# Softmax steps given out one at a time, and four values visits joined to the next scores, in a two-layer attention kernel

## The chip, the cores and the metric

The kernel runs on one core of a Trainium2 chip. The metric is device microseconds of one execution. The kernel before takes 1779.6 us, the median of three runs (1779.0 to 1781.2).

## The reference

Two attention layers of the same size (S = 2048 positions, D = 1024, 32 heads of 32) are computed from separate inputs, and their outputs are put side by side.

```python
# layer A: each position sees 8 positions back, every second one
qkv = (x @ wqkv).reshape(B, S, 3, H, Dh); q, k, v = ...      # H = 32, Dh = 32
off = jnp.arange(8) * 2
idx = pos[:, None] - off[None, :]
logits = einsum("bhsd,bhswd->bhsw", q, k[idx]) * Dh**-0.5     # masked where idx < 0
o = einsum("bhsw,bhswd->bhsd", softmax(logits), v[idx])
a = o.reshape(B, S, D) @ wo
# layer B: each position sees the 256 positions up to itself
scores = einsum("bhqd,bhkd->bhqk", q, k) * Dh**-0.5           # masked to 0 <= q - k < 256
b = einsum("bhqk,bhkd->bhqd", softmax(scores), v).reshape(B, S, D) @ wo
return concatenate([a, b], axis=-1)
```

## The kernel before

The work is cut into eight units of 512 positions: u0 to u3 are layer B, u4 to u7 layer A. For layer A the even and the odd positions are laid out as separate rows, so that "every second position" becomes a plain window of neighbours. A unit has eight groups (s0 to s7) of four heads. In the names below, u5s0 is the first group of unit 5.

Most of TensorE's time goes into three GEMMs: queries and keys (`qk_items`, matmuls at L616), values (`v_items`, L685) and the output projection (`o_items`, L749). Each number is kept as a high and a low part, and each product takes three matmuls, so matmuls come in multiples of three. A weight tile `raw` is loaded by a DMA that POOL issues (L182). Its high half is a cast, on ScalarE (L233) or on VectorE (L236), and its low half is a subtract on VectorE, two instructions of 128x512 (L239). GEMM outputs go to PSUM banks g (two of them) and x (one), and are read out from there before the bank is used again.

In layer A a group is handled by `window(u, s)`. SyncE gathers its queries and keys with eight DMAs into `pbuf` (L536). A *scores visit* of TensorE is 32 pairs of small matmuls into the four banks s (L822, 64 rows of the profile). Then comes the softmax, on a tile `band`, of which there are two, used in turn:

- VectorE adds the mask, four instructions, one for each bank (L830);
- VectorE takes the maximum (L840) and subtracts it (L842), ScalarE takes the exponential (L846);
- VectorE sums (L854), takes the reciprocal (L856), multiplies (L858), and transposes two halves (L861) into a tile `wide`;
- ScalarE copies each half into strips, four pairs of copies each (L870, L873).

A *values visit* (L896) multiplies the strips with the values of `vbuf`, one half of the rows into the bank o and the other half into a bank s. Where the table `PAIRS` names two groups, their two values visits follow each other without a break. In `overlap`, ScalarE and VectorE add what the two halves share (L994, L996), form the high and low parts (L998 to L1007), and give the banks back. A wide round of the values GEMM, 48 matmuls for two banks at a time, stands at a unit's first group.

No engine's order is found while the kernel runs: each engine executes its instructions in the order in which the program was written. A planner writes it. It keeps a model of every engine's time (`Clock`, named `ck`): `ck.use(engine, duration, ready)` books an instruction and returns its end, and `ck.defer(t, f)` has `f` called, and its instructions written, when the model's TensorE reaches time `t`. TensorE's work is a set of four queues of items; the planner takes the item that can start first by its `ready()`. Weight splits are written as the GEMM items ask for them. A function that writes several instructions at once therefore puts them next to each other on their engine, and whatever is written later stands behind them all:

```python
nc.vector.reciprocal(sm, sm)
ck.use("dve", 0.285, ck.now)
nc.vector.tensor_tensor(p16(), p16(), sm[...], op=ALU.mult)
ck.use("dve", 1.39, ck.now, port=True)
for i in range(2):
    nc.vector.transpose(turned[i], band[buf][:, 768 * i:768 * i + 768])
    e = ck.use("dve", 0.88, ck.now)
    ck.defer(e - 0.1, lambda i=i, e=e: spread(i, e))
```

Of the kernel before, what the change touches and what calls it, by code (L numbers as in the profile page):

```python
# [9 lines left out]
AF = mybir.ActivationFunctionType  # L10
# [4 lines left out]
P = 128  # L15
# [245 lines left out]
def kernel(ctx, tc, xs, wqk, wv, wo, outs, units):  # L261
# [531 lines left out]
    def window(u, s):  # L793
# [13 lines left out]

        h = pairs[hg % 2] = {}
# [29 lines left out]
        def top():  # L838
            nm = small.tile([P, 16], F32, tag="nm", name="nm")
            nc.vector.tensor_reduce(nm, p16(), axis=mybir.AxisListType.X, op=ALU.max)  # L840
            ck.use("dve", 1.39, ck.now)
            nc.vector.tensor_tensor(p16(), p16(), nm[:, :, None].to_broadcast([P, 16, 72]), op=ALU.subtract)  # L842
            e = ck.use("dve", 1.39, ck.now, port=True)

            def expo():
                nc.scalar.activation(p16(), p16(), AF.Exp)  # L846
                e2 = ck.use("act", 1.07, e)
                ck.defer(e2 - 0.1, lambda: total(e2))

            ck.defer(e - 0.1, expo)  # L850

        def total(e):
            sm = small.tile([P, 16], F32, tag="sm", name="sm")
            nc.vector.tensor_reduce(sm, p16(), axis=mybir.AxisListType.X, op=ALU.add)  # L854
# [3 lines left out]
            nc.vector.tensor_tensor(p16(), p16(), sm[:, :, None].to_broadcast([P, 16, 72]), op=ALU.mult)  # L858
            ck.use("dve", 1.39, ck.now, port=True)
            for i in range(2):  # L860
                nc.vector.transpose(turned[i], band[buf][:, 768 * i:768 * i + 768])  # L861
                e = ck.use("dve", 0.88, ck.now)
                ck.defer(e - 0.1, lambda i=i, e=e: spread(i, e))

        def spread(half, e):
            pieces = turned[half].rearrange("p (j b t c) -> p j b t c", j=2, b=4, t=3)
            diag = wide[buf][:, 2 * half:2 * half + 2].rearrange("p j (b c) -> p j b c", b=4)
            for i in range(4):
                r, c = 32 * i, 32 * i + 8
# [4 lines left out]
                t = ck.use("act", 0.255, e)  # L874
            if half:
                h["p"] = t + PACE[u][3] + HOLD[u][s]

        def values_ready():
            if len(seats_x.free) < len(both):
                return None  # L880
            return latest(done["v"].get((u, vp)), *[x.get("p") for x in both], ro.when(),
                          rs.when() if alone else rs.empty())

        def values():
            own = ro if alone or s % 2 else rs
            h["o"], first_bank = own.take()
            h["o2"], bank = rs.take()
            halves = [h["o"], h["o2"]]
# [11 lines left out]

            return lambda: overlap(u, s, h, bank, own, first_bank, 0 if has_halo else 1)

# [79 lines left out]

    def overlap(u, s, h, bank, own, first_bank, first):

# [363 lines left out]
```

## Time and profile before

| | |
|---|---|
| median of three runs | 1779.6 us |
| the profiled execution | 1781.06 us, its span 1779.3 us |
| TensorE matmuls (PE) | 1766.2 us busy, 99% |
| TensorE weight loads (PEld, beside PE) | 1474.0 us, 83% |
| VectorE (DVE) | 1260.9 us, 71% |
| ScalarE (ACT) | 1048.8 us, 59% |
| GpSimd (POOL) | 375.4 us, 21% |
| DMA | 257.51 MB, mean 145 GB/s |

Times in the profile are microseconds from the start of the span. A row of the timeline gives start, duration, engine, line, operation with its output and inputs, the shape, and how many instructions the row holds; in square brackets, the idle time before it and what ended that. The ends of matmuls are modelled, so a loss on TensorE is best read from the starts of matmuls, not from its busy share. The waits view lists for each engine what it waited for. PEclk is the clock that TensorE was granted, 1.00 being full speed. Line numbers are those of the kernel before; in the kernel after the same statements stand a little lower (L239 becomes L240, L616 L617, L685 L686, L749 L750, L822 L825, L861 L871, L896 L920).

### The profile page before, as it was taken

To read this page: it belongs to the slowest core of one execution; us is meant where nothing else is said; L and a number is where in the kernel's file an instruction comes from. 1 tells how busy PE (TensorE), PEld (TensorE's weight loads), DVE (VectorE), ACT (ScalarE), POOL (GpSimd) and SP (SyncE) were. 2 spreads that over 40 slices of the span, in tenths; PEclk is the share of its full clock that TensorE was granted. 3 is DMA by queue.
4 is the path that set the end of the run, shared out by engine and by line. 5 is a ranking of instruction groups with operands and counts; after the bars stand their busy time and mean duration, and the time that the engine had idled before them with its cause. 6 is when DMAs were issued, how large, how long until landed. Compare 5 with 4: busy or idle time off the path is not lost.

```text
span 1779.3 us, 39469 instructions
## 1 busy us (share of the span) xinstructions
PE 1766.2 (99%) x15210; PEld 1474.0 (83%) x15210; DVE 1260.9 (71%) x2690; ACT 1048.8 (59%) x2629; POOL 375.4 (21%) x829
## 2 busy tenths in 40 slices
PE   9999999999999999999999999999999999999999
PEld 7888888888888888888888888877888888888897
DVE  5678776677676779665766578776678676957873
ACT  5677766765776666676666455644455445534452
POOL 3322323224222212232233300110001100110000
PEclk9999999999999999999999999999999999999999
DMA  6656655647555556545554443433444443544432
GB/s 207 159 149 174 175 139 151 161 136 207 151 156 162 146 151 185 141 141 139 144 162 123 137 137 120 154 120 125 139 121 141 145 129 119 156 142 126 130 104 83
DMA packets 109723, 257.51 MB, mean 145 GB/s; under 512 B 14560, under 2 KB 29920, under 8 KB 109536
## 3 DMA queue, kind: packets, MB, share of 16 engines
q0 software_dynamic: 41760, 152.06, 28.5%
q1 hardware_dynamic: 58560, 86.15, 18.4%
q10 hardware_dynamic: 9216, 16.78, 2.5%
q8 instruction: 120, 1.97, 0.5%
q14 instruction: 67, 0.55, 0.1%
HBM read 164.63 MB, written 23.07 MB: 105 GB/s over the span
## 4 chain that ended last, share of the span: by engine, by line
PE 90%; DVE 3%; ACT 2%; DMA 2%; issue 2%; POOL 0%; SPq 0%; DVEq 0%; ACTq 0%; POOLq 0%
PE g L616 30%; PE g L749 16%; PE g L685 14%; PE x L616 6%; PE s L1121 6%; PE s L1037 5%; PE o L1186 3%; PE x L749 3%; PE x L685 2%; PE s L822 1%; PE x L1186 1%; DVE w L239 1%; PE s L896 1%; DMA raw<-wv 1%; DMA raw<-xs 1%
## 5 line engine op out<-in xcount | busy, mean ns | idle before, releaser
L616 PE MATMUL g<-x,w 128*128 128x512 f32 x2568 | 639.3, 392 | 0.6 <-ACT w L233 0.6
L616 PEld LDWEIGHTS g<-x,w 128*128 128x128 f32 x2568 | 475.4, 188 | 89.6 <-ACT w L233 1.0
L239 DVE TENSOR_TENSOR w<-raw,w 128x512 fp32r<-128x512 f32 x514 | 335.9, 695 | 42.8 <-ACT w L233 36.3
L1042 DVE CUSTOM_DVE_ANT_0 s<-s,mask_d 128x384 f32<-128x384 f32 (+2 forms) x512 | 262.7, 555 | 137.4 <-PE s L1037 136.2
L685 PE MATMUL g<-w,x 128*128 128x256 f32 (+1 forms) x1872 | 331.5, 320 | 0.7 <-DVE w L239 0.7
L1047 ACT ACTIVATE s<-s,nm 128x384 f32<-128x384 f32 (+2 forms) x512 | 274.1, 536 | 65.9 <-DVE nm L1042 64.7
L685 PEld LDWEIGHTS g<-w,x 128*128 128x128 f32 x1872 | 277.5, 191 | 24.5 <-DVE w L239 1.4
L749 PE MATMUL g<-ot,w 128*128 128x512 f32 x1200 | 294.5, 392 | 0.0
L749 PEld LDWEIGHTS g<-ot,w 128*128 128x128 f32 x1200 | 222.4, 188 | 43.4
L1106 POOL TENSOR_SCALAR_AFFINE_SELECT pbuf<-pbuf 128x128 f32<-128x128 f32 (+1 forms) x498 | 191.6, 412 | 202.5 <-ACT pbuf L1128 188.5
L1128 ACT ACTIVATE pbuf<-s 128x512 f32<-128x512 f32 (+1 forms) x368 | 188.9, 602 | 49.7 <-PE s L1121 48.1
L236 DVE CAST w<-raw 128x1024 fp32r<-128x1024 f32 x189 | 137.2, 726 | 77.9 <-PE g L616 27.3
L182 POOL DMA_DIRECT2D raw<-wqk x126 | 69.1, 549 | 505.0 <-DVE w L239 300.2
L1037 PE MATMUL s<-kst,qst 96*128 96x384 f32 (+2 forms) x512 | 141.1, 338 | 2.1 <-issue 1.0
L870 ACT COPY wide<-wide 32x256 f32<-32x256 f32 x256 | 103.4, 404 | 47.1 <-DVE wide L861 43.5
L1121 PE MATMUL s<-qst,kst 128*128 128x128 f32 (+2 forms) x704 | 126.1, 307 | 0.5 <-ACT pbuf L1128 0.3
L616 PE MATMUL x<-x,w 128*128 128x512 f32 x504 | 122.3, 393 | 0.0
L1121 PEld LDWEIGHTS s<-qst,kst 128*128 128x128 f32 x704 | 107.7, 189 | 15.8 <-ACT s L1047 1.7
L1037 PEld LDWEIGHTS s<-kst,qst 96*128 96x128 f32 x512 | 92.6, 189 | 22.6 <-ACT s L1047 3.1
L616 PEld LDWEIGHTS x<-x,w 128*128 128x128 f32 x504 | 93.3, 188 | 20.2
L1047 ACT ACTIVATION_READ_ACCUMULATOR s<-s,nm 128x1 f32 x512 | 105.9, 207 | 0.2
L182 POOL DMA_DIRECT2D raw<-wo x64 | 35.8, 559 | 322.8 <-DVE w L239 175.5
(114 smaller groups left out, 1907.5 us busy)
## 6 DMA issues: line engine op xcount, KB each, us to landing
raw<-wqk POOLq DMA_DIRECT2D x126, 512.0 KB, 4.0
raw<-wv POOLq DMA_DIRECT2D x72, 512.0 KB, 4.7
raw<-wo POOLq DMA_DIRECT2D x64, 512.0 KB, 4.1
qst<-nat SPq DMA_DIRECT2D x96, 256.0 KB, 4.1
kst<-nat SPq DMA_DIRECT2D x96, 256.0 KB, 5.2
raw<-xs POOLq DMA_DIRECT2D x28, 512.0 KB, 4.5
outs<-ost ACTq DMA_DIRECT2D x56, 256.0 KB, 2.5
kst<-halo SPq DMA_DIRECT2D x72, 128.0 KB, 2.8
```

Of the source, the lines that this page charges most:

```text
L182: self.nc.gpsimd.dma_start(raw if len(ap.shape) == 2 else raw.rearrange("p (a b) -> p a b", a=2), ap)
L236: nc.vector.tensor_copy(t[:, 0, :], raw)
L239: nc.vector.tensor_tensor(t[:, 1, c:c + 512], raw[:, c:c + 512], t[:, 0, c:c + 512].bitcast(F32), op=ALU.subtract)
L616: nc.tensor.matmul(h["ps"], h["w"][:, a, k * P:(k + 1) * P], xt[u][k][:, b, :], start=(k == 0 and i == 0), stop=(k == NK - 1 and i == 2))
L685: nc.tensor.matmul(ps, xt[u][kw * g + k][:, a, p0:p0 + P], h["w"][g][:, c, k], start=(first and t == 0 and half == 0), stop=(last and t == 2),
L749: nc.tensor.matmul(h["ps"], w[:, a, c:c + P], ot[u, k][:, b, :], start=(k == 0 and i == 0), stop=(k == NK - 1 and i == 2))
L1037: nc.tensor.matmul(ps[:, :n], q[0:96, j, b * P:(b + 1) * P], kk[0:96, j, c0:c1], start=True, stop=True)
L1042: nc.vector.tensor_tensor_reduce(ps[:, :n], ps[:, :n], mask[:, cut:full], scale=-1.0, scalar=BIG, op0=ALU.add, op1=ALU.min, accum_out=nm)
L1047: nc.scalar.activation(ps[:, :n], ps[:, :n], AF.Exp, bias=nm, scale=-1.0, accum_out=sm)
L1106: nc.gpsimd.affine_select(w, w, pattern=[[0, m], [step, n]], compare_op=ALU.is_ge, fill=0.0, base=base, channel_multiplier=chan)
L1121: nc.tensor.matmul(ps[:, x:x + w], kk[:, j, 256 + kb * P:256 + (kb + 1) * P], q[:, j, q0:q0 + w], start=True, stop=True)
L1128: nc.scalar.activation(w, ps[:, :m * n].rearrange("p (j n) -> p j n", j=m), AF.Exp)
```

## The change

Two things change, both in layer A.

*The steps.* `top` wrote maximum and subtract together; now the subtract is deferred to 0.15 us before the maximum's modelled end. `total` wrote sum, reciprocal, multiply and both transposes together; now the multiply is deferred to the end of the reciprocal, the first transpose to the end of the multiply, the second to the end of the first. `spread` wrote all eight copies of a half together; now each pair is deferred to the end of the pair before it. What the planner decides meanwhile (weight splits, read-outs of banks, another group's steps) is written between them.

*The chain.* A new table `CHAIN` names a group each in four places: s7 of u5, s2 and s7 of u6, s2 of u7. There the values visit waits until the next group's scores could start as well (all four s banks free, its queries and keys stacked), takes a bank g in place of a bank s for its second half, and the next group's scores follow at once.

No instruction is added or removed on any engine, and the orders of POOL and SyncE are the same.

```diff
+CHAIN = ((), (), (), (), (), (7,), (2, 7), (2,))
...
+        follows = s - 1 in CHAIN[u] if s else NG - 1 in CHAIN[u - 1]
+        leads = s in CHAIN[u]
+        h = pairs[hg % 2] = {"after": pairs[1 - hg % 2] or {}}
         def scores_ready():
-            return latest(rs.empty(), done["stack"].get((u, s)),
+            return latest(rs.empty(), done["stack"].get((u, s)), h["after"].get("run", 0.0 if not follows else None),
...
         def top():
             nc.vector.tensor_reduce(nm, p16(), axis=mybir.AxisListType.X, op=ALU.max)
-            ck.use("dve", 1.39, ck.now)
-            nc.vector.tensor_tensor(p16(), p16(), nm[:, :, None].to_broadcast([P, 16, 72]), op=ALU.subtract)
-            e = ck.use("dve", 1.39, ck.now, port=True)
+            e1 = ck.use("dve", 1.39, ck.now)
+            def less():
+                nc.vector.tensor_tensor(p16(), p16(), nm[:, :, None].to_broadcast([P, 16, 72]), op=ALU.subtract)
+                e = ck.use("dve", 1.39, ck.now, port=True)
...
+            ck.defer(e1 - 0.15, less)
...
             nc.vector.reciprocal(sm, sm)
-            ck.use("dve", 0.285, ck.now)
-            nc.vector.tensor_tensor(p16(), p16(), sm[:, :, None].to_broadcast([P, 16, 72]), op=ALU.mult)
-            ck.use("dve", 1.39, ck.now, port=True)
-            for i in range(2):
+            r = ck.use("dve", 0.285, ck.now)
+            def parts():
+                nc.vector.tensor_tensor(p16(), p16(), sm[:, :, None].to_broadcast([P, 16, 72]), op=ALU.mult)
+                ck.defer(ck.use("dve", 1.39, ck.now, port=True) - 0.15, lambda: turn(0))
+            def turn(i):
                 nc.vector.transpose(turned[i], band[buf][:, 768 * i:768 * i + 768])
                 e = ck.use("dve", 0.88, ck.now)
-                ck.defer(e - 0.1, lambda i=i, e=e: spread(i, e))
+                ck.defer(e - 0.1, lambda: spread(i, e))
+                if not i:
+                    ck.defer(e - 0.15, lambda: turn(1))
+            ck.defer(r - 0.15, parts)
...
+                if i < 3:
+                    ck.defer(t - 0.15, lambda: strip(i + 1))
...
         def values_ready():
             return latest(done["v"].get((u, vp)), *[x.get("p") for x in both], ro.when(),
+                          latest(rs.empty(), rg.when(), done["stack"].get(divmod(hg + 1, NG))) if leads else
                           rs.when() if alone else rs.empty())
         def values():
-            h["o2"], bank = rs.take()
+            other = rg if leads else rs
+            h["o2"], bank = other.take()
+            h["run"] = 0.0
...
-            rs.give(bank, e)
+            other.give(bank, e)
```

The rows of each engine's order show what moves. The first place is VectorE at the start of unit 6, where the wide round of the values GEMM runs while the softmax of the group before ends. `band` and `wide` belong to that softmax, `w` with its `raw` are weights of the round. Before:

```order
L854 TENSOR_REDUCE sm_15625<-band_11579 128x16
L856 RECIPROCAL sm_15625<-sm_15625 128x16
L858 TENSOR_TENSOR band_11579<-band_11579,sm_15625 128x16x72
L861 STREAM_TRANSPOSE wide_11312<-band_11579 128x768
L861 STREAM_TRANSPOSE wide_11581<-band_11579 128x768
L239 TENSOR_TENSOR w_15646<-raw_15539,w_15646 128x512 x2
L236 CAST w_15678<-raw_15590 128x1024
```

After:

```order
L861 TENSOR_REDUCE sm_15558<-band_11579 128x16
L863 RECIPROCAL sm_15558<-sm_15558 128x16
L524 MEMSET nat_15511 128x8
L867 TENSOR_TENSOR band_11579<-band_11579,sm_15558 128x16x72
L240 TENSOR_TENSOR w_15597<-raw_15522,w_15597 128x512 x2
L871 STREAM_TRANSPOSE wide_11312<-band_11579 128x768
L1020 TENSOR_TENSOR o_15613<-o_15613,band_11310 128x8x8
L237 CAST w_15661<-raw_15527 128x1024
L240 TENSOR_TENSOR w_15661<-raw_15527,w_15661 128x512 x2
```

The split of the round's weight (`w_15646` before, `w_15597` after) stood behind both transposes; now it stands ahead of them, and the next weight's cast and split follow between the two.

The second place is TensorE at the edge from unit 4 to unit 5. The rows `s<-pbuf` are scores visits, `g<-w,x` the wide round. Before, the scores of u5s0 stand inside that round:

```order
L896 MATMUL s<-wide,vbuf_124 32x64 x4
L616 MATMUL x<-x,w 128x512 x6
L685 MATMUL g<-w,x 128x512 x36
L822 MATMUL s<-pbuf 64x72 x32
L685 MATMUL g<-w,x 128x512 x12
L685 MATMUL x<-w,x 128x512 x3
```

After, the scores that come first here are those of u4s6 and u4s7:

```order
L686 MATMUL g<-w,x 128x256 x6
L825 MATMUL s<-pbuf 64x72 x32
L617 MATMUL g<-x,w 128x512 x12
L825 MATMUL s<-pbuf 64x72 x32
L617 MATMUL g<-x,w 128x512 x12
L617 MATMUL x<-x,w 128x512 x24
L686 MATMUL g<-w,x 128x512 x48
```

and the scores of u5s0 come later, in the next group's queries and keys:

```order
L686 MATMUL x<-w,x 128x512 x3
L686 MATMUL g<-w,x 128x512 x3
L617 MATMUL g<-x,w 128x512 x3
L825 MATMUL s<-pbuf 64x72 x32
L617 MATMUL g<-x,w 128x512 x6
```

The scores of u5s0 move behind the rest of the values GEMM, 63 GEMM matmuls and one values visit later relative to the start of the round, and the scores of u4s7 stand 12 matmuls behind those of u4s6.

VectorE at that second place, after, from the subtract of u4s6 on; `band_11310` is the softmax of u4s6 and `band_11579` that of u4s7:

```order
L847 TENSOR_TENSOR band_11310<-band_11310,nm_13314 128x16x72
L240 TENSOR_TENSOR w_13389<-raw_13295,w_13389 128x512 x2
L843 TENSOR_REDUCE nm_13393<-band_11579 128x16
L861 TENSOR_REDUCE sm_13405<-band_11310 128x16
L863 RECIPROCAL sm_13405<-sm_13405 128x16
L847 TENSOR_TENSOR band_11579<-band_11579,nm_13393 128x16x72
L867 TENSOR_TENSOR band_11310<-band_11310,sm_13405 128x16x72
L240 TENSOR_TENSOR w_13441<-raw_13352,w_13441 128x512 x2
L861 TENSOR_REDUCE sm_13449<-band_11579 128x16
L863 RECIPROCAL sm_13449<-sm_13449 128x16
L871 STREAM_TRANSPOSE wide_11312<-band_11310 128x768
L240 TENSOR_TENSOR w_13462<-raw_13367,w_13462 128x512 x2
```

The steps of the two groups alternate, and the weights of the round (`w_13389`, `w_13441`, `w_13462`) stand between them, where before one group's steps stood as blocks.

The third place is TensorE at u7s2, one of the four places in `CHAIN`. Before, nine GEMM matmuls stand between the values (L896) and the next scores (L822):

```order
L896 MATMUL o<-wide,vbuf_123 32x72 x4
L896 MATMUL s<-wide,vbuf_123 32x64 x4
L616 MATMUL x<-x,w 128x512 x9
L822 MATMUL s<-pbuf 64x72 x32
L616 MATMUL x<-x,w 128x512 x6
L749 MATMUL g<-ot,w 128x512 x42
```

After, the scores follow the values at once, and the values write to a bank g:

```order
L920 MATMUL g<-wide,vbuf_123 32x72 x4
L920 MATMUL o<-wide,vbuf_123 32x72 x4
L920 MATMUL g<-wide,vbuf_123 32x64 x4
L825 MATMUL s<-pbuf 64x72 x32
L750 MATMUL g<-ot,w 128x512 x24
L750 MATMUL x<-ot,w 128x512 x12
```

More of the change, by code (lines that the diff above doesn't have):

```diff
@@ L840, in top, with expo @@
             nc.vector.tensor_reduce(nm, p16(), axis=mybir.AxisListType.X, op=ALU.max)
-            ck.use("dve", 1.39, ck.now)
-            nc.vector.tensor_tensor(p16(), p16(), nm[:, :, None].to_broadcast([P, 16, 72]), op=ALU.subtract)
-            e = ck.use("dve", 1.39, ck.now, port=True)
[L845 to L850, printed above, removed]
+            e1 = ck.use("dve", 1.39, ck.now)
+            def less():
+                nc.vector.tensor_tensor(p16(), p16(), nm[:, :, None].to_broadcast([P, 16, 72]), op=ALU.subtract)
+                e = ck.use("dve", 1.39, ck.now, port=True)
+                def expo():
+                    nc.scalar.activation(p16(), p16(), AF.Exp)
+                    e2 = ck.use("act", 1.07, e)
+                    ck.defer(e2 - 0.1, lambda: total(e2))
+                ck.defer(e - 0.1, expo)
+            ck.defer(e1 - 0.15, less)
         def total(e):
@@ L867, in spread, with strip @@
             diag = wide[buf][:, 2 * half:2 * half + 2].rearrange("p j (b c) -> p j b c", b=4)
-            for i in range(4):
+            def strip(i):
                 r, c = 32 * i, 32 * i + 8
@@ L874, in spread @@
                 t = ck.use("act", 0.255, e)
-            if half:
-                h["p"] = t + PACE[u][3] + HOLD[u][s]
+                if i < 3:
+                    ck.defer(t - 0.15, lambda: strip(i + 1))
+                else:
+                    h["strips"] = h.get("strips", 0) + 1
+                    if h["strips"] == 2:
+                        h["p"] = t + PACE[u][3] + HOLD[u][s]
+            strip(0)
         def values_ready():
@@ L899, in values @@
                     seen.add((i, j))
-            return lambda: overlap(u, s, h, bank, own, first_bank, 0 if has_halo else 1)
+            return lambda: overlap(u, s, h, bank, other, own, first_bank, 0 if has_halo else 1)
         alone = s // 2 not in PAIRS[u]
@@ L980, in join, with overlap @@
         ck.defer(r, add)
-    def overlap(u, s, h, bank, own, first_bank, first):
+    def overlap(u, s, h, bank, other, own, first_bank, first):
         hg = u * NG + s
```

1 line of the change is left out of this document (removed).

## The prediction

> **What bounds the kernel now.** I read the page's head first, then the waits of TensorE, then the timeline around each wait they show. The page:
>
> ```profile
> span 1779.3 us, 39469 instructions
> PE 1766.2 (99%) x15210; PEld 1474.0 (83%) x15210; DVE 1260.9 (71%) x2690; ACT 1048.8 (59%) x2629; POOL 375.4 (21%) x829
> ```
>
> TensorE (PE) is busy for 1766.2 of 1779.3 us. No other engine is near that, and the change takes no instruction away, so it can gain only what PE loses, in one of three forms: a wait, a stretch in which its matmuls run slower than elsewhere, or the switch from one kind of matmul to another. The waits view of PE, whose columns are what it waited for, us in total, times, and the longest, holds these rows in layer A:
>
> ```profile
> PE x L685 <- DVE w L239: 1.6, 1, 1.6
> PE s L896 <- issue: 1.0, 1, 1.0
> PE g L685 <- DVE w L239: 0.7, 2, 0.4
> ```
>
> So PE waits for a weight's low half (L239, VectorE) three times and once for nothing that the profile shows. Waits alone understate the loss, so I also measure each place against the pace of undisturbed GEMM, which the timeline of PE gives (start, us, engine, line, operation, count):
>
> ```profile
> 1245.31 5.60 PE L749 MATMUL x<-ot,w 128*128 128x512 f32 x24
> 1250.75 4.24 PE L749 MATMUL g<-ot,w 128*128 128x512 f32 x18
> ```
>
> 24 matmuls take 1250.75 − 1245.31 = 5.44 us, 0.2267 each. A visit to the window attention is dearer than its matmuls' own time, since PE changes kind twice. The two visits at u7s2/s3 price it:
>
> ```profile
> 1642.79 2.20 PE L616 MATMUL x<-x,w 128*128 128x512 f32 x9
> 1645.76 2.33 PE L616 MATMUL x<-x,w 128*128 128x512 f32 x9
> 1648.02 0.94 PE L822 MATMUL s<-pbuf 32*64 32x72 f32 x64
> 1648.89 1.65 PE L616 MATMUL x<-x,w 128*128 128x512 f32 x6
> ```
>
> From 1642.79 to 1648.89 are 6.10 us with 18 GEMM matmuls (4.08) in them: 2.02 for a values visit and a scores visit, about 1.01 each.
>
> **The change part by part.** *Unit u5's first group.* PE at the edge from u4 to u5, then SyncE's queue, ScalarE and VectorE, then two rows of the table by windows (length, busy time of PE, PEld, DVE, ACT, POOL, granted clock, DMA share, GB/s):
>
> ```profile
> 1158.08 8.32 PE L685 MATMUL g<-w,x 128*128 128x512 f32 x36
> 1166.33 0.34 PE L822 MATMUL s<-pbuf 32*64 32x72 f32 x4
> 1168.62 0.50 PE L685 MATMUL g<-w,x 128*128 128x512 f32 x1
> 1169.37 4.37 PE L685 MATMUL g<-w,x 128*128 128x512 f32 x11 [0.26 <-DVE w L239]
> 1173.58 0.85 PE L685 MATMUL x<-w,x 128*128 128x512 f32 x3
> ```
>
> ```profile
> 1155.59 8.58 SPq L536 DMA_DIRECT2D pbuf<-nat  x8
> ```
>
> ```profile
> 1162.72 1.05 ACT L233 CAST w<-raw 128x1024 fp32r<-128x1024 f32 x1
> ```
>
> ```profile
> 1166.31 1.84 DVE L861 STREAM_TRANSPOSE wide<-band 128x768 f32<-128x768 f32 x2
> 1168.07 1.25 DVE L239 TENSOR_TENSOR w<-raw,w 128x512 fp32r<-128x512 f32 x2
> ```
>
> ```profile
> 1166.33:1169.90 3.57, 2.48 (x68) 1.80 (x68) 3.57 (x6) 2.50 (x8) 0.02 (x1) 1.00 0.14 37
> 1169.90:1173.30 3.40, 3.40 (x9) 2.65 (x9) 3.33 (x5) 3.22 (x10) 0.53 (x1) 0.50 0.53 154
> ```
>
> From 1158.08 to 1173.58 are 15.50 us. In them lie 48 matmuls (10.88) and one scores visit (1.07 with its share of the last, longer triplet): 3.55 are lost, in three ways. The gather that feeds these scores (L536) was still being issued until 1164.17, and PE stalls inside the visit. Then the weight whose cast ended at 1163.77 gets its low half only at 1168.07, since the softmax of the other group stands ahead of it on VectorE as one block that ends with the two transposes. Then the clock is halved for 3.40 us, which costs 1.7: it follows a stretch in which PE was busy 2.48 of 3.57 us.
>
> [...]
>
> In the new order these scores stand 63 GEMM matmuls and one visit later relative to the round of values GEMMs (L685): 63 × 0.2267 + 1.01 = 15.3 us, against a gather that was late by about 1. The first stall goes: −3.55 with what followed it. What is late next: the round itself now runs 48 matmuls without a visit, four weights of 12, while two groups' softmaxes (u4s6 and u4s7, now 12 matmuls apart) share VectorE with those weights. From the end of u4s7's scores to the last weight's low half VectorE has, in the new order, four masks (0.4 each, an estimate: a quarter of the elements of the multiply quoted for u6 below), three reduces (1.37), two subtracts and a multiply (1.39 each, with the gap to the next step), two reciprocals (0.3), one transpose (0.92) and three splits (1.3): 1.6 + 4.1 + 4.2 + 0.6 + 0.9 + 3.9 = 15.3. PE asks for that weight 72 matmuls after the scores, 16.3. A cover of 1.0, from which any wait of VectorE for the exponentials is taken; between 0 and the whole 3.55 I take +0.5.
>
> *Unit u6's first group.* The timeline of PE, ScalarE and VectorE:
>
> ```profile
> 1360.43 0.39 PE L685 MATMUL x<-w,x 128*128 128x512 f32 x1
> 1362.40 0.73 PE L685 MATMUL x<-w,x 128*128 128x512 f32 x2 [1.58 <-DVE w L239]
> ```
>
> ```profile
> 1355.73 1.06 ACT L233 CAST w<-raw 128x1024 fp32r<-128x1024 f32 x1
> ```
>
> ```profile
> 1356.28 1.34 DVE L854 TENSOR_REDUCE sm<-band 128x16 f32<-128x1152 f32 x1
> ...
> 1357.94 1.36 DVE L858 TENSOR_TENSOR band<-band,sm 128x1152 f32<-128x1152 f32 x1
> 1359.33 1.84 DVE L861 STREAM_TRANSPOSE wide<-band 128x768 f32<-128x768 f32 x2
> 1361.10 1.25 DVE L239 TENSOR_TENSOR w<-raw,w 128x512 fp32r<-128x512 f32 x2
> ```
>
> PE's next matmul starts 1362.40 − 1360.43 = 1.97 late less one pace, 1.74. The cast ended at 1356.79; the low half waited for reduce, reciprocal, multiply and both transposes, 4.8 us. In the new order the low half stands ahead of the transposes: it would run from 1359.33 to 1360.6, and PE asks at 1360.66. Gain 1.74. Behind it the next weight has a transpose (0.92), a small addition (64 elements a partition, taken as no longer than ScalarE's 0.40 for 256, quoted further below), its cast (no longer than ScalarE's 1.06) and its low half (1.25) to go, 3.6 us at most, and PE asks for it 12 matmuls (2.72) on. Ends 0 and 0.9, taken +0.4.
>
> *Unit u7's first group*, the same pattern, smaller:
>
> ```profile
> 1554.33 0.39 PE L685 MATMUL g<-w,x 128*128 128x512 f32 x1
> 1555.14 0.73 PE L685 MATMUL g<-w,x 128*128 128x512 f32 x2 [0.43 <-DVE w L239]
> ```
>
> 1555.14 − 1554.33 − 0.23 = 0.58, and it goes: −0.58.
>
> *The wait without a releaser*, in a visit for two groups' values in u5:
>
> ```profile
> 1222.04 0.92 PE L896 MATMUL s<-wide,vbuf 64*32 64x8 f32 x76
> 1224.77 0.30 PE L896 MATMUL s<-wide,vbuf 64*32 64x64 f32 x4 [1.04 <-issue]
> 1225.01 3.06 PE L749 MATMUL g<-ot,w 128*128 128x512 f32 x12
> 1268.15 6.28 PE L749 MATMUL g<-ot,w 128*128 128x512 f32 x27
> 1274.37 0.92 PE L896 MATMUL s<-wide,vbuf 64*32 64x8 f32 x76
> 1275.94 5.05 PE L749 MATMUL g<-ot,w 128*128 128x512 f32 x21
> ```
>
> The visit took 1225.01 − 1222.04 = 2.97 and its twin 1275.94 − 1274.37 = 1.57: 1.40 lost. Nothing released it, so I read it as PE's own instructions not being there, which the page's queue 8 carries:
>
> ```profile
> q8 instruction: 120, 1.97, 0.5%
> ```
>
> 1.97 MB in 120 packets is 16 KB a packet. Such a stall would hang on where the long visit falls in the stream, and in the new order this visit starts 12 instructions further on. Of the long visits of this kernel this one alone shows it, so I book −1.40; its other end is 0.
>
> [...]
>
> *The four joined visits.* The two groups' values in one run cost, from 1268.15 to 1275.94, 7.79 less 27 matmuls (6.12): 1.67, where two visits apart cost 2.02. Joining is worth 0.35 by that row, but in the new pairs the second half is scores, which read other operands; between 0 and 0.45 I take 0.3: −1.2 for four.
>
> *What the joining asks for.* The values' second half now takes a GEMM bank (g) at these places and gives it back when VectorE has formed the low half (L1004). At u5s7 and u6s7 it is taken within rounds whose tiles change bank every three matmuls (0.68), so the next g tile is due in 1.36 us. No row of before shows this; it is bounded by 0 and by the longest wait for an eviction-like step on PE, the 1.6 above. Nearer to 0, since two tiles' time covers it: +0.2 each at two places, +0.4. Behind a waiting PE all is queued. The joined values also wait for the four score banks and the next group's stack, and the scores wait for the values' turn; those scores move at most a few us and the order of SyncE's and POOL's queues is unchanged.
>
> *Steps given out singly, elsewhere.* A weight or an eviction slipped between steps makes that group's values later. The waits view shows no PE wait on the strip copies in before, so this is new cost:
>
> ```profile
> L870 ACT COPY wide<-wide 32x256 f32<-32x256 f32 x256 | 103.4, 404 | 47.1 <-DVE wide L861 43.5
> ```
>
> Between 0 and one copy of 0.40 at each of some six tightest of 25 visits (2.4), I take +0.6. The other way, a weight that comes sooner, gains nothing where PE does not wait.
>
> *Sum*, against the profiled execution's own 1781.06 (span 1779.3 and 1.76 around it): removed 3.55 + 1.74 + 0.58 + 1.40 = 7.27, joined 1.2; added 0.5 + 0.4 + 0.4 + 0.6 = 1.9. 1781.06 − 7.27 − 1.2 + 1.9 = 1774.5. That execution is 1.5 above the median of 1779.6, so a median may come out nearer 1773; I take 1774.0.
>
> **The rivals.** (1) *The edges stay late.* The round's weights are as late as before because the steps that let them through bring the second softmax in: only the joins and the 1.40 are gained, 1781.06 − 2.6 = 1778.5, within 0.2%. For it speaks the 1.0 us of cover at u5; against it u6, where the order plainly moves the split ahead. Chance 0.16.
>
> (2) *The joined visits outrun the instructions.* A joined run is nearly as long as the visit that stalled; if each of the four loses 1.4, 5.6 come back: 1774.5 + 5.6 = 1780.1, within 0.2%. Against it: the twin visit of the same length ran free. [...] Chance 0.07.
>
> (3) *Slower: half clock at all three edges.* If the two interleaved softmaxes hold a weight back by 2.5 us at each of u5, u6 and u7, and each such gap brings 1.7 of half clock as it did at 1169.90, the edges cost 3 × 4.2 = 12.6 against the 3.55 + 1.74 + 0.58 = 5.87 lost there now. With the joins and the 1.40 kept that is 1781.06 − 2.6 − 5.87 + 12.6 = 1785.2. It decides from 10.6 us at the edges (1783.2). For it: the first edge did just this. Against: the steps now let a split in between each. Chance 0.17.
>
> That the change does nothing is excluded: the order on PE has four pairs of visits adjacent that were apart.
>
> **How the numbers follow.** Forecast 0.60, rivals 0.16, 0.07 and 0.17. 0.2% of 1779.6 is 3.6 us, about what a measurement of this kernel can tell: faster means under 1776.0, slower over 1783.2. Of the forecast I leave 0.02 in the middle. Faster 0.58, same 0.25, slower 0.17. The range: downward no added cost and joins at 0.45, 1781.06 − 7.27 − 1.8 = 1772.0, and the run spread below the profiled execution (1781.06 to 1779.0) puts it at 1770.0; upward it takes in rivals 1 and 2 and the upper ends of the unknown costs, to 1781.0.
>
> **What would show it.** Right: in the profile after, no wait for L240 (the old L239) at the starts of u5, u6, u7, no half clock after the first microseconds, no gap without a releaser in a values visit, and joined visits at about 1.7 to 1.8 us. Wrong: PE waiting for a g bank behind VectorE's release at u5s7 or u6s7, PE waiting for strip copies, a granted clock under 1.00 at an edge, or a new gap in a joined visit.

## The result and the profile after

The kernel after takes 1777.73 us (median of 14 runs, 1775.36 to 1781.61), the kernel before 1780.35 (14 runs, 1778.79 to 1781.42). The medians differ by 2.6 us; the ratio is 0.9984, 95% interval 0.9977 to 0.9991. That is inside the range that was given and on the side that was forecast, but 3.7 us above the forecast of 1774.0 and inside the 0.2% called "same".

The page of the profile after, and rows of the waits of TensorE:

```profile
span 1776.3 us, 39487 instructions
PE 1764.9 (99%) x15210; PEld 1473.9 (83%) x15210; DVE 1239.7 (70%) x2662; ACT 1068.8 (60%) x2657; POOL 372.9 (21%) x829
```

```profile
PE s L920 <- ACT wide L888: 1.4, 1, 1.4
...
PE s L686 <- DVE w L240: 0.8, 1, 0.8
PE x L750 <- DVE ot L1031: 0.4, 1, 0.4
```

VectorE has 28 instructions fewer than before and ScalarE 28 more. The planner also chooses which of the two engines does a weight's cast or reads out a bank, and in the new order it gave ScalarE 18 casts and 10 read-outs more. So it isn't true, as was said ahead of the prediction, that no instruction is added or removed on any engine: VectorE is busy for 21.2 us less and ScalarE for 20.0 us more. No run holds that choice fixed, so its share in what follows is not shown.

The three waits for a weight's low half in layer A are gone (the one for L240 that is left lies at 26 us, in layer B). Two waits are new: a values visit waits for strips, and the output projection for `ot`. The timeline of TensorE shows the starts of u5, then the visit for two groups in u5, then the joined visit at the start of u6:

```profile
1160.06 11.04 PE L686 MATMUL g<-w,x 128*128 128x512 f32 x48
1170.94 0.84 PE L686 MATMUL x<-w,x 128*128 128x512 f32 x3
...
1223.03 0.92 PE L920 MATMUL s<-wide,vbuf 64*32 64x8 f32 x76
...
1224.61 1.66 PE L750 MATMUL g<-ot,w 128*128 128x512 f32 x6
```

```profile
1366.11 0.84 PE L686 MATMUL x<-w,x 128*128 128x512 f32 x3
1366.88 0.21 PE L920 MATMUL g<-wide,vbuf 64*32 64x8 f32 x4
...
1367.73 1.12 PE L825 MATMUL s<-pbuf 32*64 32x72 f32 x64
1368.78 0.96 PE L686 MATMUL g<-w,x 128*128 128x512 f32 x3
```

The 48 matmuls of u5's round start at 1160.06 and the next at 1170.94: 10.88 us, the plain pace, where the same work with one visit lost 3.55 before. The visit at 1223.03 takes 1.58 (it took 2.97). The joined visit takes from 1366.88 to 1368.78, 1.90 us; apart, values and scores take 0.84 and 0.87, 1.71. Counted from the due end of the last GEMM matmul ahead of it and with the triplet behind it, which is 0.11 longer, the joined visit costs 2.10, and two apart 2.11: no gain.

One fault of the kernel after has to be known before its time is read: in three groups of u4 some strips are copied from the next group's softmax, which the kernel before never does. The experiment "The transposes in turn" shows where, and what the time is without it.

A measure that recurs below is *layer A*: the time from the start of the first scores visit to the start of the last matmul. In the profile before it is 753.85 us, in the profile after 749.43.

### The profile page after: what moved, and what is told of

Its sections match the earlier page's. It is cut to its first block, busy times and chain, and to the rows that moved or that the text cites. A ratio compares the mean times of both kernels' runs of the same rounds, so it can differ in the third digit from the quotient of the medians.

```text
span 1776.3 us, 39487 instructions
## 1 busy us (share of the span) xinstructions
PE 1764.9 (99%) x15210; PEld 1473.9 (83%) x15210; DVE 1239.7 (70%) x2662; ACT 1068.8 (60%) x2657; POOL 372.9 (21%) x829
## 3 DMA queue, kind: packets, MB, share of 16 engines
q8 instruction: 120, 1.97, 0.5%
## 4 chain that ended last, share of the span: by engine, by line
PE 95%; ACT 2%; DVE 1%; DMA 1%; issue 0%; POOL 0%; SPq 0%; POOLq 0%; ACTq 0%; DVEq 0%
PE g L617 32%; PE g L686 16%; PE g L750 15%; PE s L1145 6%; PE x L617 6%; PE s L1061 5%; PE x L750 4%; PE o L1210 3%; PE x L686 3%; PE s L825 2%; PE x L1210 1%; PE s L920 1%; PE o L920 1%; ACT s L1071 0%; ACT qst L1106 0%
## 5 line engine op out<-in xcount | busy, mean ns | idle before, releaser
L617 PE MATMUL g<-x,w 128*128 128x512 f32 x2640 | 656.8, 392 | 1.0 <-ACT w L234 1.0
L617 PEld LDWEIGHTS g<-x,w 128*128 128x128 f32 x2640 | 488.8, 188 | 92.8 <-ACT w L234 1.5
L240 DVE TENSOR_TENSOR w<-raw,w 128x512 fp32r<-128x512 f32 x514 | 335.7, 695 | 52.7 <-ACT w L234 46.5
L750 PE MATMUL g<-ot,w 128*128 128x512 f32 x1128 | 276.6, 392 | 0.0
L750 PEld LDWEIGHTS g<-ot,w 128*128 128x128 f32 x1128 | 209.2, 188 | 40.6
L237 DVE CAST w<-raw 128x1024 fp32r<-128x1024 f32 x176 | 128.1, 728 | 68.4 <-PE g L617 24.9
L617 PE MATMUL x<-x,w 128*128 128x512 f32 x432 | 103.6, 392 | 0.0
L183 POOL DMA_DIRECT2D raw<-wv x72 | 46.3, 643 | 255.3 <-DVE w L240 123.3
```

Of the source, the lines that this page charges most:

```text
L183: self.nc.gpsimd.dma_start(raw if len(ap.shape) == 2 else raw.rearrange("p (a b) -> p a b", a=2), ap)
L237: nc.vector.tensor_copy(t[:, 0, :], raw)
L240: nc.vector.tensor_tensor(t[:, 1, c:c + 512], raw[:, c:c + 512], t[:, 0, c:c + 512].bitcast(F32), op=ALU.subtract)
L617: nc.tensor.matmul(h["ps"], h["w"][:, a, k * P:(k + 1) * P], xt[u][k][:, b, :], start=(k == 0 and i == 0), stop=(k == NK - 1 and i == 2))
L750: nc.tensor.matmul(h["ps"], w[:, a, c:c + P], ot[u, k][:, b, :], start=(k == 0 and i == 0), stop=(k == NK - 1 and i == 2))
```

## The experiments

Each kernel was timed beside runs of the kernel before; times below are medians, and layer A is from the one profiled execution.

| kernel | time, us | ratio to before, 95% | layer A, us |
|---|---|---|---|
| before; again | 1780.35; 1780.1 (one run) | | 753.85; 751.49 |
| after; again | 1777.73; 1778.10 | 0.9984 (0.9977 to 0.9991); 0.9983 (0.9974 to 0.9991) | 749.43; 749.11 |
| steps only | 1778.04 | 0.9980 (0.9971 to 0.9989) | 749.75 |
| chain only | 1781.77 | 1.0006 (0.9997 to 1.0015) | 752.81 |
| after, transposes in turn | 1778.87 | 0.9991 (0.9982 to 1.0000) | 749.88 |
| second half of the softmax only | 1780.52 | 0.9995 (0.9986 to 1.0004) | 753.25 |
| steps, strips as a block | 1776.24; 1775.70 | 0.9972 (0.9961 to 0.9984); 0.9972 (0.9961 to 0.9982) | 746.79; 746.93 |
| the same with the chain | 1775.95 | 0.9971 (0.9960 to 0.9983) | 747.07 |
| steps, strips as a block, late masks | 1774.00 | 0.9963 (0.9951 to 0.9976) | 747.37 |
| before, 6 warm-ups more | 1777.74 (one run) | | 750.73 |
| before, 5 warm-ups fewer | 1783.14 (one run) | | 753.03 |

**The steps alone.**

```diff
-CHAIN = ((), (), (), (), (), (7,), (2, 7), (2,))
+CHAIN = ((), (), (), (), (), (), (), ())
```

> The steps given out singly, with the table CHAIN empty, so no values visit is joined to the next scores. Theory A (the four losses of before went through the steps alone, and a join of values and scores is worth nothing, 0.01 us each by the after profile, 2.10 joined against 2.11 apart): as the kernel after within 0.5 us, about 2.6 us below before; no wait for a weight's low half at the starts of u5, u6 and u7; the values visit of u4s2 again waits about 1.4 us for its strips, since u4 has no join in either kernel. Theory B (the joins are worth 0.3 each as predicted): 1.2 us slower than the kernel after, about 1.4 below before.

1778.04 against 1777.73 and 1778.10 for the kernel after: the same. The three waits at the starts of u5, u6 and u7 are gone as in the kernel after (a values visit in u7 takes 0.48 longer), and u4s2 loses the same 1.68. Theory A holds, and the joins are worth nothing here.

**The chain alone.** `top`, `total` and `spread` as in the kernel before, CHAIN as after.

> The joins alone, with the softmax steps written as blocks as in the kernel before. Theory A: the losses at the starts of u5 (3.6 us), u6 (1.7) and u7 (0.6) stay or return, the joins bring 0, so it is within 0.8 us of before, less up to 1.4 if the two-group visit in u5 falls elsewhere in the instruction stream (its order up to there is that of before, so it should keep its gap of 1.0). Theory B: 1.2 us below before by the four joins.

1781.77 beside 1780.77 for the kernel before, interval 0.03% under to 0.15% over: no gain, so theory B falls a second time. The 1.0 us above before is a little more than the 0.8 that theory A allowed, and not clear of the noise. Its waits view has the losses of before back:

```profile
PE x L686 <- DVE w L240: 1.7, 1, 1.7
...
PE g L686 <- DVE w L240: 0.8, 2, 0.6
```

**The transposes in turn.** The two tiles that the transposes write are shared by both groups. In the kernel after three pairs of groups in u4 have the next group's transpose ahead of strip copies of the group before. The timelines of TensorE, ScalarE and VectorE there, after:

```profile
1096.84 0.23 PE L920 MATMUL s<-wide,vbuf 64*32 64x72 f32 x2
1098.49 0.25 PE L920 MATMUL s<-wide,vbuf 64*32 64x72 f32 x2 [1.43 <-ACT wide L888]
```

```profile
1091.40 0.40 ACT L885 COPY wide<-wide 32x256 f32<-32x256 f32 x1 [2.25 <-DVE wide L871]
```

```profile
1090.40 0.97 DVE L871 STREAM_TRANSPOSE wide<-band 128x768 f32<-128x768 f32 x1
1094.75 0.98 DVE L871 STREAM_TRANSPOSE wide<-band 128x768 f32<-128x768 f32 x1 [3.38 <-ACT wide L888]
```

ScalarE stands still for 2.25 us until the next group's transpose is done, VectorE then 3.38 until strips have been read, and TensorE 1.43 inside the visit.

The order costs more than time. A copy that is written behind the next group's transpose reads what that transpose has put into the tile. By the order in which the instructions are written, 20 of the 512 strip copies of the kernel after (in u4s0, u4s2 and u4s6) copy the next group's softmax in place of their own; in the kernel before, none does. The steps alone have the same 20. With the inputs of the reference the logits are near zero (a standard deviation of 0.006, an estimate from the scale of the inputs), every softmax weight is near one eighth, and the output hardly changes; with other inputs these heads would be wrong. The next kernel puts the order right.

```diff
             def turn(i):
+                if unread[i]:
+                    return ck.defer(ck.now + 0.2, lambda: turn(i))
+                unread[i] = 4
...
                 t = ck.use("act", 0.255, e)
+                unread[half] -= 1
```

> The kernel after, but a group's transpose into one of the two shared tiles is written only when all four strip pairs of the group before have been written for that tile. In the kernel after three pairs of groups in u4 have the next group's transpose ahead of the last strips, so that these strips wait for it and copy the next group's numbers; here they copy their own. Theory A (that order is what makes the values visit of u4s2 wait): the 1.4 us wait for a strip copy in u4 goes, layer A is 1.7 us shorter than in the kernel after, about 4.3 us below before. Rival C (the strips are late because two softmaxes and the weights fill ScalarE and VectorE there, and the order only shifts which of them is late): the wait stays above 1 us in u4, at that visit or at the next, and the time is that of the kernel after.

The wait at u4s2 went, and others came: the timeline of TensorE has

```profile
1164.80 3.01 PE L686 MATMUL g<-w,x 128*128 128x512 f32 x12 [0.25 <-DVE w L240]
...
1168.76 2.79 PE L686 MATMUL g<-w,x 128*128 128x512 f32 x11 [0.95 <-DVE w L240]
...
1178.63 0.25 PE L926 MATMUL s<-wide,vbuf 64*32 64x72 f32 x2 [0.68 <-ACT wide L893]
```

Layer A is 749.88, not 747.7, and the time 1778.87 beside 1778.10 for the kernel after. That is nearest to rival C: what went at u4s2 came back at u5's round and at the values visit of u4s6. This is the only kernel with the new steps whose strips are all copied from their own group, and beside before it is 1.9 us faster, with an interval of 0 to 3.2. It also shows how thin the cover at u5's round is, since a shift of the softmaxes by a few steps gives 0.25 + 0.95 of wait there.

**The kernel after again.**

> The kernel after once more, unchanged, to see what differs between its executions, whose times spread over 6 us (1775.4 to 1781.6) where those of before spread over 2.6. Theory A: the layer A part of the timeline repeats within 0.5 us and the differences lie in the first 40 us, where TensorE waits for the first loads. Rival D: some executions have a half-clock spell behind the strip wait in u4, 1.7 us each, and layer A differs by that.

Layer A is 749.11 and 749.43, every place within 0.15 us, and no half clock between the first 6 us and the end in either, the granted clock being 1.00 there: theory A as far as layer A goes, and nothing for D. What spread the first fourteen times over 6 us isn't shown; these eleven lie between 1776.84 and 1778.73.

**The second half of the softmax only.** Multiply and transposes given out singly, maximum with subtract and the strips as blocks.

> Only the second half of the softmax is given out singly (multiply, transpose, transpose); maximum and subtract, and the eight strip copies of a half, stay blocks; CHAIN is empty. Theory A (the waits at the starts of u5, u6 and u7 came from the block that ends in two transposes, and the strips given out singly only cost): all three waits go and the strip wait in u4 too, layer A about 748 us against 749.1 to 749.4 in the kernel after, so 1.5 us faster than the kernel after. Rival C (as the mended order showed, a wait taken away at one place of u4 or u5 comes back at another): layer A stays within 0.5 of 749.5.

Wrong for theory A: layer A is 753.25, in an execution that was the slowest of its eleven and 2.3 us above their median. u5's round waits 0.5 and 1.1 us for low halves, and at the start of u6 the queries and keys wait for a cast (timeline of TensorE, then the table by windows):

```profile
1350.00 2.22 PE L617 MATMUL g<-x,w 128*128 128x512 f32 x5 [1.88 <-ACT w L234]
```

```profile
1346.00:1350.90 4.90, 3.02 (x13) 1.90 (x12) 4.58 (x6) 4.58 (x11) 0.00 (x0) 1.00 0.04 16
1350.90:1354.30 3.40, 3.40 (x9) 2.63 (x10) 3.33 (x6) 3.33 (x8) 1.44 (x2) 0.50 0.39 89
```

So the gain of the steps is not one cut block; it hangs on where all of a group's steps fall, maximum and subtract too. In this kernel 32 strip copies, all of u4s2 and u4s6, read the next group's softmax.

**The strips as a block.**

```diff
                 if i < 3:
-                    ck.defer(t - 0.15, lambda: strip(i + 1))
+                    strip(i + 1)
```

with CHAIN empty; run twice.

> As with the steps alone, CHAIN empty, but the eight strip copies of a half are written as a block again. Theory A: the 1.4 us strip wait in u4 goes, nothing else changes: layer A about 748. Rival C: it stays within 0.5 of 749.5, with the wait at another place.

> The steps given out singly, strip copies as a block, no joins, once more beside the other kernels of this call: 1776.2 us was its median of six runs. Expected within 0.5 of that, layer A 746.8 within 0.5.

1776.24 and 1775.70, layer A 746.79 and 746.93: theory A, and 1.2 us shorter than it asked for. In layer A one row is left in the waits of TensorE:

```profile
PE g L686 <- DVE w L240: 0.2, 1, 0.2
```

But this kernel is not a sound one either. The timelines of VectorE and ScalarE at the edge from u4 to u5:

```profile
1168.18 3.85 DVE L871 STREAM_TRANSPOSE wide<-band 128x768 f32<-128x768 f32 x4
```

```profile
1170.36 0.40 ACT L885 COPY wide<-wide 32x256 f32<-32x256 f32 x1
```

The four transposes of u4s6 (`band_11310`) and u4s7 (`band_11579`) follow each other without a wait, and the order of VectorE has them in turn into the same two tiles:

```order
L871 STREAM_TRANSPOSE wide_11312<-band_11310 128x768
L871 STREAM_TRANSPOSE wide_11312<-band_11579 128x768
L871 STREAM_TRANSPOSE wide_11581<-band_11310 128x768
L871 STREAM_TRANSPOSE wide_11581<-band_11579 128x768
```

The strip copies of u4s6 begin at 1170.36, when the second transpose has overwritten what the first had put there; all 16 of them read the softmax of u4s7. What this kernel, and the two below that are built on it, would take with the order put right was not run.

**The same with the chain.**

> The kernel after with the eight strip copies of a half written as a block: steps and joins, no singly given strips. Theory A (a join of values and scores is worth nothing): within 0.5 us of the same kernel without joins, which runs beside it. Theory B (0.3 for each join): 1.2 us faster than that. Rival H (the joins hold a GEMM bank and wait for more, and cost): 0.5 us or more slower.

1775.95 beside 1775.70, layer A 747.07 beside 746.93: nothing gained or lost. Theory A, for the third time.

**The place in the instruction stream.** The page of the kernel before has 30420 matmuls and weight loads to the 120 packets of queue 8, 253.5 a packet; with the semaphore instructions of TensorE its trace has 255.6 from the first packet to the last. Places are counted in blocks of 256 instructions of TensorE's stream, an estimate from these numbers; where a block begins is not shown. Six small matmuls more, or five warm-ups fewer, at the start of the kernel before:

```diff
+        for i in range(6):
+            nc.tensor.matmul(ps[:, :64], idle[:, :P], idle[:, :64], start=True, stop=True)
         for i in range(WARM):
```

```diff
-        for i in range(WARM):
+        for i in range(WARM - 5):
```

> The kernel before with six small matmuls (64 columns) added to the ten that warm TensorE up at the start: every later instruction of TensorE stands 12 places further on in its stream, and nothing else moves. Theory F (the gap without a releaser in u5's two-group visit is instructions that come late, and hangs on where the visit starts in the 256-instruction blocks: 168 in before): at 180 the gap of 1.0 to 1.4 us goes and the visit takes 1.57 to 1.7. Rival G (the gap comes from what the visit waits for, its operands or banks): it stays at about 1 us. Also one more sample of u5's first group: if the half-clock spell of 3.4 us that the profiled execution of before showed is not there, it belongs to some executions only.

> The kernel before with five of its ten warm-up matmuls left out: every later instruction of TensorE stands 10 places earlier. Theory F: the two-group visit in u7 moves from place 178 of its block to 168, and gets a gap of 0.6 to 1.4 us that it did not have; that of u5 moves from 168 to 158, where the same gap falls at its end or just behind it. Rival G: u7's visit stays at 1.6 to 1.75 us and u5's keeps its gap. One more sample of the half-clock spell at u5's first group.

Twelve places on, u5's visit for two groups takes 1221.99 − 1220.34 = 1.65 and has no gap (timeline of TensorE with six more):

```profile
1220.34 0.92 PE L896 MATMUL s<-wide,vbuf 64*32 64x8 f32 x76
...
1221.99 3.01 PE L749 MATMUL g<-ot,w 128*128 128x512 f32 x12
```

Ten places back, the gap follows one GEMM matmul behind the visit (with five fewer):

```profile
1224.42 0.92 PE L896 MATMUL s<-wide,vbuf 64*32 64x8 f32 x76
1226.03 0.50 PE L749 MATMUL g<-ot,w 128*128 128x512 f32 x1
1227.45 2.68 PE L749 MATMUL g<-ot,w 128*128 128x512 f32 x11 [0.92 <-issue]
```

A gap that goes, or leaves the visit, when nothing but the place in the stream changes is not a matter of the visit's operands: rival G falls. The other traces agree. The visit in u5 stands within two places of 168 in the chain alone and in the second half only as well, and takes 2.23 and 1.97 there; in the nine executions in which it stands at least eight places further on it takes 1.57 to 1.67. Theory F holds for u5 only: the visit in u7, put at place 168 by the second kernel, took 1.57 and had no gap, and at place 172 it took 2.06 in the steps alone, with 0.26 without a releaser. The place is a condition, then, and not the only one; what else decides stays open. That the instructions come late is still a reading: no view shows when they arrive.

The kernel with six matmuls more took 1777.74 in its one run, as little as the kernel after. Its layer A, 750.73, is 0.8 below that of the kernel before again, for the gap alone, and 1.3 to 1.6 above the kernel after.

**The kernel before again.**

> The kernel before once more, unchanged. Its half-clock spell of 3.4 us at 1170 was not in three other kernels that have the same gaps there. If spells belong to some executions only, it is absent here with a chance of about 3 in 4, and layer A is about 752.1 instead of 753.85; the gap in u5's two-group visit stays, 0.6 to 1.4 us.

No half clock, and layer A 751.49. The stretches that correspond to those of the prediction, from the start of the scores visit on, by windows, in the kernel before again and then with five warm-ups fewer:

```profile
1167.78:1171.35 3.57, 3.02 (x71) 2.22 (x71) 3.57 (x8) 3.02 (x10) 0.55 (x1) 1.00 0.04 10
1171.35:1174.75 3.40, 2.92 (x13) 2.13 (x12) 3.05 (x3) 3.28 (x10) 0.00 (x0) 1.00 0.53 154
```

```profile
1169.14:1172.71 3.57, 2.09 (x67) 1.46 (x67) 3.54 (x6) 2.12 (x7) 0.00 (x0) 1.00 0.26 72
1172.71:1176.11 3.40, 3.30 (x14) 2.41 (x14) 3.33 (x6) 3.27 (x11) 0.55 (x1) 1.00 0.47 143
```

In the kernel before again the waits at u5 are there, though shorter in the visit (0.86 in the scores visit, 0.55 and 0.64 behind it, 2.04 in all), and the clock stays at 1.00. With five warm-ups fewer the visit loses more than in the profile before, 1.82 against 1.42, TensorE is busy for only 2.09 of 3.57 us, and the clock stays at 1.00 all the same. Of the five profiled executions in which u5 starts as it did before (before twice, its two variants with other warm-ups, the chain alone), one has the spell. The gap in the visit is 0.92 here instead of 1.40.

**Late masks.** Between the loads of weights at the start, GpSimd makes small masks, among them eight selects of 32x4.

```diff
-(17.0, turns)
+(20.0, turns)
```

on top of the steps with strips as a block.

> The same kernel, with the small masks that GpSimd makes at the start (a memset, a select of 128x128 and eight selects of 32x4) given out after the fifth load of values weights instead of after the third; the orders of TensorE and VectorE are the same. Theory S (the first scores visit of layer A comes 0.7 to 1.8 us later in five of the changed kernels than in the kernel before since those eight selects take 4.7 to 4.9 us in them, 4.2 in before, and hold back the load for which TensorE waits 1.1 us at 26 us): the wait of 1.1 us at 26 us goes, 1 us faster than the kernel beside it, the first scores visit near 1021.5. Rival: the load is late for DMA reasons, the wait stays.

1774.00 beside 1775.70, five runs within 0.7 us (1773.46 to 1774.16) beside seven within 2.7, each of the five below each of the seven, and no wait near 26 or 27 us. The profiled execution beside it happens to lack that wait too (and took 1774.20, against 1774.09 here), so the 1.7 is shown by the medians and not row by row. The timelines of GpSimd, VectorE and TensorE in the kernel before again, then of TensorE in the late masks:

```profile
14.59 4.85 POOL L385 TENSOR_SCALAR_AFFINE_SELECT pick<-pick 32x4 f32<-32x4 f32 x8
```

```profile
25.05 0.69 DVE L236 CAST w<-raw 128x1024 fp32r<-128x1024 f32 x1 [2.57 <-DMA raw<-wv]
```

```profile
27.13 2.11 PE L685 MATMUL s<-w,x 128*128 128x512 f32 x8 [0.83 <-DVE w L239]
```

```profile
22.62 6.74 PE L686 MATMUL s<-w,x 128*128 128x512 f32 x29
```

The theory as written was wrong in one point: the long selects do not belong to the changed kernels. The unchanged kernel before has them too (4.85), and the same changed kernel took 4.83 in one execution and 3.57 in another. The 1.1 of the expectation is this wait of 0.83 with a shorter one ahead of it, in those executions that have both. Over all fourteen profiles the wait of 0.82 or 0.83 is there in the seven whose selects took 4.66 or more. In the six at 4.24 or less it is 0.34 at most, and in the late masks, where the selects stand elsewhere, there is none. This version was the fastest of all, with the fault in u4s6 that it has from the kernel under it.

## Why the prediction was right or wrong

**The sign and the mechanism of the steps were right.** The low halves do get between the steps, the gather is early enough, and the waits at u5, u6 and u7 go with the steps alone (shown by the steps alone and the chain alone). The thin cover of 1.0 at u5, booked at +0.5, cost nothing in the kernel after; the +0.4 at u6 cost nothing either. Of the prediction's own signs of being wrong one came true, TensorE waiting for strip copies, and one of its signs of being right did not: the joined visits took 1.86 to 1.90, not 1.7 to 1.8.

**The size was wrong, in three terms.** Against its own execution the forecast promised 1781.06 − 1774.0 = 7.1, against the median of 14 runs 6.4, and the runs gave 2.6. That the time still fell inside the range owes something to luck: the range reached up to rivals 1 and 2, and the errors in the terms did not pass it.

*The removed 7.27 was mostly that, but in one execution.* Read in the second profile of the kernel before, the same four places cost 2.04 + 1.77 + 0.16 + 0.92 = 4.9. The largest part of the difference is the half clock, 1.5 of the 3.55 at u5, which one of five executions had; the gap and u7's wait were also at their larger values. The step that failed is "−3.55 with what followed it": one profile's spell was taken for a fixed cost. The prediction saw that the median lay 1.5 below the profiled execution, and lowered its forecast by 0.5 for that; it was a sign that the loss itself was smaller. The 0.92 of the gap went as booked, but by the visit's new place in the stream, as it did with six matmuls more in the kernel before, and not by what the change is about.

Of the executions with the same order at u5, one has the spell and four have not. What brings it is not shown: the stretch before the spell in the prediction was 69% busy (2.48 of 3.57), and a stretch 59% busy (2.09 of 3.57) brought no spell in another execution.

*The joins were worth 0, not 1.2.* The price of 0.35 was read from two values visits in one run. A values visit and a scores visit in one run keep the whole cost of both (2.10 against 2.11). Two pairs of kernels with and without the chain agree within 0.4 us, and in the third, the chain alone beside before, the chain is not faster. The prediction's remark that the second half of the new pairs "is scores, which read other operands" named the risk, and its price stayed near that row all the same.

*The added 1.9 was 3.0, and in other places.* The bank g held by the joins, +0.4, shows at most 0.16 at u7. The waits for strips, +0.6 for all, were 1.67 at one place: not one copy late, but strips queued behind another group's transposes in a tile that both share. The prediction priced a late copy and did not ask what else may be written between two steps; nothing in the planner keeps the next group's transpose behind these copies, and so some of them also copy the wrong numbers. And the projection's wait for `ot` near the end was not in the sum:

```profile
1731.89 0.73 PE L750 MATMUL x<-ot,w 128*128 128x512 f32 x2 [0.39 <-DVE ot L1031]
```

```profile
1729.82 1.35 DVE L847 TENSOR_TENSOR band<-band,nm 128x1152 f32<-128x1152 f32 x1
1731.09 0.38 DVE L1028 TENSOR_TENSOR ot<-s,ot 128x224 fp32r<-128x224 f32 x1
1731.39 0.45 DVE L1031 TENSOR_TENSOR ot<-o,ot 128x288 fp32r<-128x288 f32 x1
```

Here the step that slipped in is itself in the way: a subtract stands ahead of the low halves of `ot`, and TensorE loses 0.55 by its pace. Together with small ones the kernel after loses 1.67 + 0.55 + 0.30 + 0.16 + 0.16 + 0.10 + 0.09 = 3.0, and 4.9 − 3.0 = 1.9 is near the 2.1 to 2.4 by which layer A is shorter than in the second profile of before, and inside the interval of the measured gain (1.6 to 4.1). The small ones were counted in the kernel after alone, so this sum is a rough one.

**The rivals.** The time came out near rival 1's 1778.5, but not by its mechanism: the edges did not stay late. Rival 2: no joined visit of the kernel after shows a gap; a visit for two groups in u7 is 0.15 to 0.30 longer than its like (0.49 in the steps alone). Rival 3 did not happen.

## What to carry to other kernels

Giving out a chain of steps singly lets urgent work in, and lets everything else in too: it paid on VectorE, where weights waited behind a block, and cost on ScalarE, where the strip copies were themselves the urgent work. What gets in may also be wrong: where two chains share a tile, a step of one that is written ahead of the other's last read changes what that read finds, so a chain that is cut up needs a rule for each tile that it shares. Before a loss read from one profile goes into a sum, look whether the runs' median already lies below that execution, and book what may be missing from other executions, a clock spell above all, at less than its face value. A price for joining two visits holds for the two kinds of visit from which it was read.

## What the runs showed of the hardware

The granted clock fell to one half for 3.4 us behind a stretch with 2.48 of 3.57 us busy, and behind 3.02 of 4.90 in another kernel, but not in four other executions with waits at the same place, one of them with 2.09 of 3.57 us busy. TensorE lost 0.4 to 1.4 us to a gap without a releaser in u5's visit of 288 instructions in all four executions in which that visit starts within two places of 168, and 0.92 one matmul behind it in the one in which it starts ten places earlier; in the nine in which it starts eight or more places further on there was no gap. That its instructions come late there is the reading that fits, and no view shows it directly. Eight tiny selects on GpSimd took 3.5 to 4.9 us from execution to execution (the profile's spans on GpSimd are rough), and where they took over 4.6, a load issued behind them came late and TensorE waited 0.8 us.
